# Last 64 score rows of two attention units at once, in quarters of the TensorE array

## The chip, the cores and the metric

The kernel runs on one core of a Trainium2 chip. The metric is the device time of one execution in microseconds. Three runs of the kernel before gave 938.68, 938.79 and 940.41 us; the median, 938.79 us, is the time that the change is compared with. All times here are microseconds unless ns is written.

## What is computed

Three stages follow one another. The first is attention with a memory, for B = 4 batches, H = 8 heads, S = 576 tokens and D = 64:

```python
scores = scale * np.matmul(q, k.transpose(0, 1, 3, 2))
scores = np.where(causal, -1000000000.0, scores)
a = np.exp(scores - scores.max(-1, keepdims=True))
a /= a.sum(-1, keepdims=True) + 1e-09
local = np.matmul(a, v)
q_p = np.where(q > 0, q, np.exp(q) - 1.0) + 1.0
mem_out = einsum(q_p, M_prev) / (einsum(q_p, z_prev)[..., None] + 1e-06)
g = 1.0 / (1.0 + np.exp(-beta))
x = g * mem_out + (1 - g) * local
```

The result is laid out as 2304 tokens x 512. Then `softplus(x @ w_in) @ w_out` with a hidden width of 2048, and then `((x @ w_a) * (x @ w_b)) @ w_out2` with a hidden width of 1536. All of it is fp32; the inputs of the attention and w_in are drawn with a spread 8 times larger than usual.

## The kernel before, in words

**A planner orders everything.** The program does not issue instructions as it is written. Each call (`PE.matmul`, `V.tensor_tensor`, `SP.dma_start`, ...) records a `Step` in a `Plan`. `Plan.weigh` (L157) gives each step a cost in a model of the chip, and `Plan.order` (L207) plays the steps through a list schedule: of what is ready, each engine takes the step with the largest `rank`, the longest modelled way to the end; PE takes its steps strictly in program order inside a stream. Stream 0 is the attention and has precedence over stream 1, the two dense stages. The result is one fixed order for each of PE (TensorE), DVE (VectorE), ACT (ScalarE), POOL (GpSimd) and SP (the queue that issues the DMAs). On the chip each engine keeps to this order and waits where a semaphore makes it wait; a step that is late holds up all that stands behind it on its engine. For DMAs of SP the planner has one limit, `LANES` (L33, L241): it issues the next one only when the sixth last one has landed in the model. DMAs on ACT's queue have no such limit.

**Attention** (`attention`, L657, and `Unit`, L454). A unit is one batch and two heads; there are 16, and the two heads hold the two halves of the 128 partitions. The loop runs over n = 0 to 17 and works on three units at once: `cur` = unit n, `prev` = unit n-1, `old` = unit n-2. In program order one turn of the loop is:

- `cur.score` (L504): q k^T of the first 512 rows, in tiles of 128 rows. q and k are each split into two fp32r parts (`qh`, `ql`, `kh`, `kl`), and three products are added up. The two heads use the upper and the lower half of the array at the same time (64*128). DVE then masks and takes the maximum (L514), ACT exponentiates and sums (L518).
- `prev.memory` (L547): phi(q) times M and z, in plain fp32, which is two instructions for one matmul.
- `nxt.prep_k` (L472): POOL and ACT split q and k of the next unit. SP loads unit n+2 (`loads_k`, L458) into one of two buffers each for `kr` and `qr`, and v.
- `old.use` and `old.finish` (L619, L635 to L652): probabilities times v, times the softmax scale that lies in `rb`, and the store to `xs`.
- `cur.score_tail` (L522): the last 64 rows. The two heads' q stand in one 128x128 block with zeros outside the diagonal (`qt[..., 512:640]`, L1171 to L1175), so that the whole array gives both heads: two chunks of 288 columns, three fp32r products each, six matmuls a unit (L531). Then one DVE pass (L532) and one ACT pass (L536).
- `cur.sums`, `cur.over` (L574, L579): POOL adds 1e-9 to the sums, DVE inverts them: `rs`, one column for each block of rows.
- `prev.send` (L558): PE turns `rs` (L562), DVE copies it (L563), SP stores it to DRAM (`rsd`, L565) and loads it back spread over 64 partitions for each head (`rb`, L568).
- `prev.turn` five times and `prev.turn_tail`: PE turns the probabilities (L589, L606, L607), ACT or DVE copies them out of PSUM (L595, L597, L609). The PSUM banks for this are the ring 4, 5, 2, 3.
- `prev.spread` (L627): the memory part is turned into the output's bank.

**The dense stages** read `xs` back, split it into fp32r parts (`right_parts`, L766) and multiply by a seven-product scheme (`Seven`, L807; L850 is its matmul). The weights come as raw 64-bit words: `decode` (L725) loads one matrix part of 1 MB with one DMA and unpacks it on DVE and ACT. `left_parts` (L755) does this for `w_in`; the first two are worked on POOL (`e` = G), their raw loads stand on ACT's DMA queue and wait for the second unit's q split (`begun`). All others load on SP.

Of the kernel before, what the change touches and what calls it, by code (L numbers as in the profile page):

```python
# [9 lines left out]
F32 = mybir.dt.float32  # L10
# [21 lines left out]
START, CONST, WORDS = 6272, 1280, 55680  # L32
SWITCH, LANES = 190, 6  # L33

# [18 lines left out]
class Plan:  # L53
# [153 lines left out]
    def order(self):  # L207
# [22 lines left out]
        while done < len(steps):  # L230
            nxt = float("inf")
            moved = False
            for e in engines:
# [4 lines left out]
                if free[e] > t:  # L238
                    nxt = min(nxt, free[e])
                    continue  # L240
                if e == "SP" and now[e] and len(landed) >= LANES and landed[-LANES] > t:  # L241
                    nxt = min(nxt, landed[-LANES])
                    continue
# [74 lines left out]
def tile_kernel(ctx: ExitStack, tc: tile.TileContext, qt, kt, vt, mz, be, w_in, w_out, w_a, w_b, w_2, out):  # L318
# [72 lines left out]
    early, late, spare = space(X1), space(X2), space(SUMS)  # L391
    for n, words in (("kr", S), ("qr", 640), ("qh", 640), ("ql", 640), ("kh", S), ("kl", S), ("ph", 640)):
        put(n, words, early(words), early(words), dtype=F32R if n[1] in "hl" and n != "ph" else F32)
    put("pos", 640, early(640))
    w3 = [early(512) for _ in range(3)]
    put("eTrue", 512, *w3, spare(512), *(late(512) for _ in range(4)))
    put("eFalse", 256, *(spare(256) for _ in range(4)), *(late(256) for _ in range(4)))
    put("eT", 640, spare(640), late(640))
    put("vr", 640, late(640), spare(640), spare(640))
# [32 lines left out]
    def gates():  # L432
        A.activation(out=gt, in_=bt, func=AF.Exp, scale=-1.0)
        G.tensor_scalar(out=gt, in0=gt, scalar1=1.0, scalar2=1.0, op0=ALU.mult, op1=ALU.add)
        V.reciprocal(out=gt, in_=gt)
        pairs = gt.rearrange("p (n j) -> p n j", j=2)
        for j, r in enumerate(both):
            rnd(G, gp[r], pairs[r, :, j])
        G.tensor_scalar(out=og, in0=gt, scalar1=-1.0, scalar2=1.0, op0=ALU.mult, op1=ALU.add)
# [13 lines left out]

    class Unit:  # L454
        def __init__(self, b, p):
            self.b, self.p = b, p

        def loads_k(self):  # L458
# [13 lines left out]
        def prep_k(self, first=False):  # L472
            kr, qr = self.kr, self.qr
            self.qh, self.ql, self.kh, self.kl = (take(n) for n in ("qh", "ql", "kh", "kl"))
            e = V if first else G
            for c, d in ((0, 256), (256, 640)) if first else ((0, 640),):
                k, q = slice(c, min(d, S)), slice(c, d)
                rnd(e, self.kh[:, k], kr[:, k])
                self.begun = {A.activation(out=self.qh[:, q], in_=qr[:, q], func=AF.Copy).n}
                sub(e, self.kl[:, k], kr[:, k], f(self.kh[:, k]))  # L480
                sub(e, self.ql[:, q], qr[:, q], f(self.qh[:, q]))
# [12 lines left out]
        def score(self, k, *rows):  # L494
# [4 lines left out]
            for i in rows:  # L499
                L = 128 * (i + 1)  # L500
                qc = slice(128 * i, 128 * i + 128)
                for t, (a, b) in enumerate(((qh, kh), (qh, kl), (ql, kh))):
                    for j, r in enumerate(both):
                        PE.matmul(  # L504
# [17 lines left out]
        def score_tail(self, k):  # L522
            qh, ql, kh, kl, sm, mn, Es = self.qh, self.ql, self.kh, self.kl, self.sm, self.mn, self.E
            s = bank[:, k : k + 2]
            terms = ((qh, kh), (qh, kl), (ql, kh))
            e640 = take("eT")
            e = e640[:, 0:S]
            for c in range(2):
                cs = slice(288 * c, 288 * c + 288)
                for t, (a, b) in enumerate(terms):  # L530
                    PE.matmul(out=s[:, c, :288], lhsT=a[:, 512:640], rhs=b[:, cs], start=t == 0, stop=t == 2)  # L531
            V.tensor_tensor_reduce(  # L532
# [3 lines left out]
            A.activation(out=e, in_=e, func=AF.Exp, scale=-1.0, bias=mn[:, 4:5], accum_out=sm[:, 4:5])  # L536
            Es["t"] = e640

        def memory(self, k):
# [5 lines left out]
            for c in range(5):  # L545
                for j, r in enumerate(both):
                    PE.matmul(  # L547
# [84 lines left out]
        def finish(self):  # L632
# [16 lines left out]
            while done < S:  # L649
# [3 lines left out]
                done += n  # L653

    order = [Unit(b, p) for b in range(B) for p in range(NP)]

    def attention():  # L657
# [16 lines left out]
        for n in range(nu + 2):  # L674
            cur, prev, old, nxt = (at(n - d) for d in (0, 1, 2, -1))
            if cur:
                cur.begin()
                cur.score(2, 2)
                cur.score(0, 0, 1)
                cur.score(4, 3)  # L680
# [17 lines left out]
            if cur:  # L698
                cur.score_tail(0)
                cur.sums()  # L700
                cur.over()
            if prev:
                rings["psT"][1] = 0
                if old:
                    prev.send(bank[0:10, 3, 0:128])
                prev.turn(A, [(0, 0)])
# [4 lines left out]
                prev.turn_tail()  # L711
                if not old:
                    prev.send(bank[0:10, 3, 0:128])
                prev.spread()

    attention()


# [5 lines left out]

    def decode(src, to, step=4, q=SP):  # L725

        raw = take("raw").bitcast(U32).rearrange("p (m c) -> p m c", c=2)
        q.dma_start(out=raw, in_=src).deps.update(order[1].begun if q is A else ())
        four = lambda t: t.rearrange("p (b n) -> p b n", b=4)
# [25 lines left out]
    def left_parts(src, at, e=V):  # L755

        w, d = (t.rearrange("p (n h m) -> p n h m", n=7, h=2) for t in twice("w", 3584, at))
        d = d[:, :, 1]
        decode(src, d[:, 0:4], 2, SP if e is V else A)
        left_sums(*(d[:, n] for n in range(7)), e)  # L760
# [447 lines left out]
```

## Time and profile before

| | us |
|---|---|
| median of three runs (lowest, highest) | 938.79 (938.68, 940.41) |
| the profiled execution, its own time | 940.39 |
| its span in the trace | 938.6 |
| PE busy in the span | 922.6 (98%) |
| DVE busy | 791.1 (84%) |
| ACT busy | 566.8 (60%) |
| POOL busy | 103.0 (11%) |

The profiled execution's span is read from the first to the last event on the core; 1.8 us lie outside it. "Busy" of PE is the time in which at least one matmul is in flight; matmuls overlap, so two that run at once count once. PEclk is the clock that TensorE was granted, as a share of 2.4 GHz. In the chain and wait views an arrow names what released an instruction. Queue names: SPq and ACTq are the sequencers of SP and ACT issuing DMAs.

### The profile page before, as it was taken

What the parts mean: (1) busy time and instruction counts of PE and PEld (TensorE: products, weight loads), DVE (VectorE), ACT (ScalarE), POOL (GpSimd) and SP (SyncE); (2) the same over time, 40 slices, a digit from 0 to 9 for tenths busy, and PEclk for the clock granted to TensorE, in tenths of its full rate; (3) what the DMA queues carried; (4) which work ended last, traced back from release to release, by engine and by line L of the source; (5) the groups of instructions that cost most, each with busy time, mean ns of one, the idle gap of its engine ahead of it and who ended that gap; (6) DMA issues with size and microseconds to landing.
All of it is one profiled execution on the core that took longest, in us unless ns stands there. A gap on an engine that the chain in (4) does not pass through costs nothing.

```text
span 938.6 us, 16918 instructions
## 1 busy us (share of the span) xinstructions
PE 922.6 (98%) x6204; PEld 890.1 (95%) x6204; DVE 791.1 (84%) x1503; ACT 566.8 (60%) x1124; POOL 103.0 (11%) x137
## 2 busy tenths in 40 slices
PE   7989999999999999999999999999999999999998
PEld 6878788899999999999999999999999999999998
DVE  7969989979998946998679999999997566998683
ACT  8968999757766756754446555544444334555452
POOL 6434588200000000000000000000000000000000
PEclk9999999999999999999999999999999999999999
DMA  6654564376988899482641444466654146672701
GB/s 185 193 162 131 169 186 130 99 232 215 312 292 293 267 329 370 172 299 73 202 135 34 134 157 159 159 226 208 224 188 144 43 160 192 245 234 74 225 32 50
DMA packets 81378, 172.10 MB, mean 183 GB/s; under 512 B 7936, under 2 KB 60560, under 8 KB 76048
## 3 DMA queue, kind: packets, MB, share of 16 engines
q1 hardware_dynamic: 80576, 168.61, 54.4%
q10 hardware_dynamic: 720, 2.43, 0.7%
q8 instruction: 48, 0.79, 0.3%
q14 instruction: 34, 0.28, 0.1%
HBM read 110.90 MB, written 60.10 MB: 182 GB/s over the span
## 4 chain that ended last, share of the span: by engine, by line
PE 86%; DVE 5%; ACT 3%; DMA 3%; issue 1%; POOL 1%; SPq 0%; DVEq 0%; POOLq 0%; ACTq 0%
PE bank L850 46%; PE bank L994 33%; DMA rb<-rsd 2%; PE bank L619 1%; PE bank L504 1%; PE bank L589 1%; PE bank L547 1%; DVE eTrue L514 1%; ACT eTrue L518 1%; PE bank L531 1%; ACT eFalse L518 1%; DMA kr<-kt 1%; PE bank L606 1%; PE bank L627 0%; ACT aT L595 0%
## 5 line engine op out<-in xcount | busy, mean ns | idle before, releaser
L340 DVE TENSOR_TENSOR s<-bank,s 128x384 f32<-128x384 f32 x216 | 117.2, 552 | 44.9 <-PE bank L850 38.9
L828 ACT ACTIVATE s<-bank 128x384 f32<-128x384 f32 x72 | 35.1, 487 | 73.2 <-PE bank L850 43.1
L337 DVE TENSOR_TENSOR t<-t,t 128x1536 f32<-128x1536 f32 (+1 forms) x48 | 74.5, 1552 | 0.4
L850 PE MATMUL bank<-x1h,w 128*128 128x384 f32 x240 | 71.0, 335 | 0.0
L850 PE MATMUL bank<-x6h,w 128*128 128x384 f32 x240 | 70.7, 335 | 0.3 <-ACT s L825 0.3
L850 PE MATMUL bank<-x5h,w 128*128 128x384 f32 x240 | 70.5, 334 | 0.0
L850 PE MATMUL bank<-x2h,w 128*128 128x384 f32 x240 | 70.5, 334 | 0.0
L850 PE MATMUL bank<-x3h,w 128*128 128x384 f32 x240 | 70.5, 334 | 0.0
L850 PE MATMUL bank<-x7h,w 128*128 128x384 f32 x240 | 70.5, 334 | 0.0
L850 PE MATMUL bank<-x4h,w 128*128 128x384 f32 x240 | 70.5, 334 | 0.0
L330 ACT ACTIVATE w<-wf 128x256 fp32r<-128x256 f32 (+1 forms) x100 | 50.0, 500 | 20.4 <-DVE w L337 16.4
L886 ACT ACTIVATE s<-s 128x384 f32<-128x384 f32 x72 | 37.2, 523 | 33.0 <-DVE s L340 32.9
L825 ACT ACTIVATE s<-bank 128x384 f32<-128x384 f32 x72 | 35.1, 487 | 35.8 <-PE bank L850 22.9
L330 ACT ACTIVATE gx2h<-t 128x768 fp32r<-128x768 f32 x37 | 31.4, 848 | 35.9 <-PE bank L994 32.7
L337 DVE TENSOR_TENSOR w<-wf,w 128x256 fp32r<-128x256 f32 (+1 forms) x90 | 47.2, 525 | 5.5 <-ACT w L330 4.9
L330 ACT ACTIVATE gx1h<-t 128x768 fp32r<-128x768 f32 x37 | 31.3, 846 | 33.4 <-PE bank L994 33.4
L734 ACT ACTIVATE raw<-raw 128x512 f32<-128x512 f32 (+1 forms) x54 | 42.6, 802 | 12.4 <-DVE raw L733 12.1
L330 ACT ACTIVATE gx0h<-t 128x768 fp32r<-128x768 f32 x37 | 31.3, 846 | 29.4 <-PE bank L994 28.5
L337 DVE TENSOR_TENSOR gx0l<-t,gx0h 128x768 fp32r<-128x768 f32 x37 | 35.3, 954 | 14.2 <-ACT gx0h L330 13.9
L518 ACT ACTIVATE eTrue<-eTrue,mn 128x384 f32<-128x384 f32 (+1 forms) x64 | 42.1, 660 | 8.2 <-DVE mn L514 8.0
L337 DVE TENSOR_TENSOR gx1l<-t,gx1h 128x768 fp32r<-128x768 f32 x37 | 35.3, 954 | 13.2 <-ACT gx1h L330 13.1
L831 ACT ACTIVATE s<-bank 128x384 f32<-128x384 f32 x72 | 35.1, 488 | 18.6 <-PE bank L850 14.6
(344 smaller groups left out, 3040.7 us busy)
## 6 DMA issues: line engine op xcount, KB each, us to landing
gs<-s SPq DMA_DIRECT2D x96, 192.0 KB
t<-gs SPq DMA_DIRECT2D x24, 768.0 KB
us<-s SPq DMA_DIRECT2D x72, 192.0 KB
t<-us SPq DMA_DIRECT2D x12, 768.0 KB
raw<-w_out SPq DMA_DIRECT2D x8, 1024.0 KB
raw<-w_in SPq DMA_DIRECT2D x6, 1024.0 KB
raw<-w_a SPq DMA_DIRECT2D x6, 1024.0 KB
raw<-w_b SPq DMA_DIRECT2D x6, 1024.0 KB
```

Source lines behind the costliest of these rows:

```text
L330: A.activation(out=o, in_=i, func=AF.Copy)
L337: eng.tensor_tensor(out=o, in0=a, in1=b, op=ALU.subtract)
L340: eng.tensor_tensor(out=o, in0=a, in1=b, op=ALU.add)
L504: PE.matmul(out=s[:, j, at : at + L], lhsT=a[r, qc], rhs=b[r, 0:L], start=t == 0, stop=t == 2, skip_group_check=True,)
L518: A.activation(out=e, in_=e, func=AF.Exp, scale=-1.0, bias=mn[:, n : n + 1], accum_out=sm[:, n : n + 1])
L734: A.activation(out=f(high), in_=f(high), func=AF.Identity, scale=REBIAS)
L825: A.activation(out=self.s1, in_=bank["b"], func=AF.Copy)
L828: A.activation(out=self.s5, in_=bank["c"], func=AF.Copy)
L831: A.activation(out=self.s2, in_=bank["b"], func=AF.Copy)
L850: PE.matmul(out=o, lhsT=w(n, a, k), rhs=x[n][c][:, k], start=start and k == t == 0, stop=k == 1 and t == 2, skip_group_check=True,)
L886: A.activation(out=s, in_=s if bank is None else bank, func=AF.Softplus)
L994: PE.matmul(out=o, lhsT=self.w[n][a][:, u, 128 * m : 128 * m + 128], rhs=x[c][:, j], start=start and u == t == 0, stop=u == self.nu - 1 an ...
```

## The change

It is one change in five parts.

1. `score_tail` no longer multiplies. A new function `tails` computes the last 64 rows of two units, n and n+1, at once, in every even turn of the loop. It uses `qr` and `kr` as loaded, in plain fp32, and gives each head of each unit a quarter of the array (64 rows x 64 columns). For an odd unit the heads change halves of q, k, memory and v input (`self.rows`), so that the four quarters are all different. The two units write to banks 0, 1 and 4, 5, the two heads of a unit to the two halves of the same bank.
2. In odd turns there is no tail. `qh` and `ql` shrink from 640 to 512 columns; `kr` and `qr` get a third buffer each, `eT` a third.
3. An odd unit's `send` stands at the end of its own turn of the loop. An even unit's stays where it is. The PSUM banks of the turning follow a ring of six that differs between even and odd turns, and the two `send`s use banks 0 and 5 in place of 3.
4. `decode` loads the raw weights in pieces: four of 256 KB for the first two `w_in` parts, which now stand on SP without the wait for `begun`; two of 512 KB for the other weights that are split in place; the weights that are spilled to DRAM are still loaded whole.
5. The planner gets a second limit for SP: when the most urgent DMA is a large one (over 300 ns of transfer in the model), it is held back while the modelled transfers already queued reach over 500 ns ahead.

```diff
-SWITCH, LANES = 190, 6
+SWITCH, LANES, AHEAD = 190, 6, 500
+TAIL = 4
+SEND, SENDC = 0, 5
+RINGS = [2, 3, 0, 1, 4, 5], [4, 5, 2, 3, 0, 1]
...
+                if e == "SP" and now[e] and steps[now[e][0][1]].size > 300 and lane[e] > t + AHEAD:
+                    nxt = min(nxt, lane[e] - AHEAD)
+                    continue
...
-    for n, words in (("kr", S), ("qr", 640), ("qh", 640), ("ql", 640), ("kh", S), ("kl", S), ("ph", 640)):
-        put(n, words, early(words), early(words), dtype=F32R if n[1] in "hl" and n != "ph" else F32)
+    more = space(WL + 7168)
+    for n, words in (("kr", S), ("qr", 640), ("qh", 512), ("ql", 512), ("kh", S), ("kl", S), ("ph", 640)):
+        at = [early(words), early(words)] + [more(words)] * (n in ("kr", "qr"))
+        put(n, words, *at, dtype=F32R if n[1] in "hl" and n != "ph" else F32)
...
-    put("eT", 640, spare(640), late(640))
+    put("eT", 640, spare(640), late(640), spare(640))
...
-        for j, r in enumerate(both):
-            rnd(G, gp[r], pairs[r, :, j])
+        for odd in range(2):
+            for j, r in enumerate(both):
+                rnd(G, gp[r, odd::2], pairs[r, odd::2, j ^ odd])
...
+            self.rows = [(h, both[h ^ (p & 1)]) for h in range(2)]
...
         def score_tail(self, k):
...
-            for c in range(2):
-                cs = slice(288 * c, 288 * c + 288)
-                for t, (a, b) in enumerate(terms):
-                    PE.matmul(out=s[:, c, :288], lhsT=a[:, 512:640], rhs=b[:, cs], start=t == 0, stop=t == 2)
...
+    def tails(at):
+        for c in range(2):
+            for u, k in at:
+                for j, r in u.rows:
+                    PE.matmul(
+                        out=bank[both[j], k + c, :288], lhsT=u.qr[r, 512 + 64 * j : 576 + 64 * j], rhs=u.kr[r, 288 * c : 288 * c + 288],
+                        start=True, stop=True, skip_group_check=True,
+                    )
+        for u, k in at:
+            u.score_tail(k)
...
             if cur:
-                cur.begin()
+                if n % 2 == 0:
+                    cur.begin()
...
             if cur:
-                cur.score_tail(0)
+                if n % 2 == 0:
+                    nxt.begin()
+                    tails(((cur, 0), (nxt, TAIL)))
                 cur.sums()
                 cur.over()
             if prev:
-                rings["psT"][1] = 0
-                if old:
-                    prev.send(bank[0:10, 3, 0:128])
+                rings["psT"] = [RINGS[n % 2], 0]
+                if n % 2:
+                    prev.send(bank[0:10, SEND, 0:128])
...
-                if not old:
-                    prev.send(bank[0:10, 3, 0:128])
                 prev.spread()
+                if cur and n % 2:
+                    cur.send(bank[0:10, SENDC, 0:128])
...
-    def decode(src, to, step=4, q=SP):
+    def decode(src, to, step=4, load=4):
         raw = take("raw").bitcast(U32).rearrange("p (m c) -> p m c", c=2)
-        q.dma_start(out=raw, in_=src).deps.update(order[1].begun if q is A else ())
+        for b in range(0, 1024, 256 * load):
+            m = slice(b, b + 256 * load)
+            SP.dma_start(out=raw[:, m], in_=src[:, m])
...
-        decode(src, d[:, 0:4], 2, SP if e is V else A)
+        decode(src, d[:, 0:4], 2, 2 if e is V else 1)
```

The host side changes to match: for odd units the heads' order is reversed in v, beta and the rows of w_in, and the last 64 rows of q change halves.

## Rows read from the trace of the kernel before

**Rows 1.** The page's first part: busy time, share of the span, instructions.

```profile
PE 922.6 (98%) x6204; PEld 890.1 (95%) x6204; DVE 791.1 (84%) x1503; ACT 566.8 (60%) x1124; POOL 103.0 (11%) x137
```

**Rows 2.** Stretches: busy time (instructions) of PE, PEld, DVE, ACT, POOL; clock; DMA share; GB/s.

```profile
80.00:90.00 10.00, 10.00 (x117) 8.44 (x116) 9.37 (x33) 7.94 (x24) 4.30 (x8) 1.00 0.46 150
...
150.00:160.00 10.00, 10.00 (x112) 8.21 (x112) 8.73 (x29) 10.00 (x29) 8.74 (x10) 1.00 0.54 167
200.00:300.00 100.00, 100.00 (x579) 100.00 (x578) 93.08 (x175) 69.32 (x140) 0.00 (x0) 1.00 0.84 277
```

**Rows 3.** Timeline of PE, the scale's turn (L562) of five loop turns: start, duration.

```profile
38.80 0.27 PE L562 MATMUL bank<-ident,rs 128*10 128x128 f32 x1
...
65.57 0.27 PE L562 MATMUL bank<-ident,rs 128*10 128x128 f32 x1
...
98.76 0.27 PE L562 MATMUL bank<-ident,rs 128*10 128x128 f32 x1
...
111.13 0.27 PE L562 MATMUL bank<-ident,rs 128*10 128x128 f32 x1
...
176.64 0.27 PE L562 MATMUL bank<-ident,rs 128*10 128x128 f32 x1
```

**Rows 4.** Timeline of PE, the last 64 rows of one unit.

```profile
27.12 0.40 PE L531 MATMUL bank<-kh,qh 128*128 128x288 f32 x1
27.36 0.29 PE L531 MATMUL bank<-kl,qh 128*128 128x288 f32 x1
...
28.02 0.27 PE L562 MATMUL bank<-ident,rs 128*10 128x128 f32 x1
```

**Rows 5.** Timeline of PE, other shares of the array.

```profile
24.12 2.37 PE L619 MATMUL bank<-aT,vr 128*64 128x512 f32 x16
26.32 0.64 PE L639 MATMUL bank<-aT,vr 128*64 128x64 f32 x16
...
33.18 0.39 PE L504 MATMUL bank<-kl,qh 64*128 64x512 f32 x2
33.41 0.40 PE L504 MATMUL bank<-kh,ql 64*128 64x512 f32 x2
```

**Rows 6.** Timelines of ACTq, SPq, DVE and PE around the first stall.

```profile
41.34 0.82 ACTq L728 DMA_DIRECT2D raw<-w_in  x2
...
42.92 1.25 SPq L568 DMA_DIRECT2D rb<-rsd  x2
...
52.78 0.69 DVE L635 TENSOR_TENSOR xx<-bank,rb 128x512 f32<-128x512 f32 x1 [1.47 <-DMA rb<-rsd]
...
54.76 0.33 PE L589 MATMUL bank<-ident,eFalse 128*128 128x128 f32 x1 [3.59 <-DVE rt L563]
```

**Rows 7.** Two stretches at the first stall, columns as in rows 2.

```profile
50.00:52.00 2.00, 1.17 (x11) 0.93 (x9) 0.22 (x1) 1.02 (x2) 0.00 (x0) 1.00 1.11 227
56.00:58.00 2.00, 2.00 (x11) 1.83 (x9) 1.05 (x3) 0.84 (x2) 1.79 (x3) 0.50 0.03 8
```

**Rows 8.** SP's own waits to 200 us; timelines of SPq and PE at the second stall.

```profile
SPq L463 <- POOL kl L337: 13.8, 7, 3.3
...
93.32 0.87 SPq L775 DMA_DIRECT2D raw<-xs  x1
94.28 1.09 SPq L568 DMA_DIRECT2D rb<-rsd  x2
...
103.25 0.33 PE L607 MATMUL bank<-ident,eT 128*128 128x128 f32 x1 [1.25 <-DVE xx L647]
```

**Rows 9.** Timelines of ACT, POOL and PE at the end of a loop turn.

```profile
37.95 0.19 ACT L518 ACTIVATION_READ_ACCUMULATOR eFalse<-eFalse,mn 128x1 f32 x1
...
41.20 1.55 POOL L337 TENSOR_TENSOR ql<-qr,qh 128x640 fp32r<-128x640 f32 x1
43.92 0.48 POOL L574 TENSOR_SCALAR ss<-sm 128x9 f32<-128x9 f32 x2 [1.18 <-DVE mn L514]
...
42.21 0.45 PE L504 MATMUL bank<-kh,qh 64*128 64x384 f32 x2
```

More of the change, by code (lines that the diff above doesn't have):

```diff
@@ L476, in prep_k @@
             for c, d in ((0, 256), (256, 640)) if first else ((0, 640),):
-                k, q = slice(c, min(d, S)), slice(c, d)
+                k, q = slice(c, min(d, S)), slice(c, min(d, 512))
                 rnd(e, self.kh[:, k], kr[:, k])
-                self.begun = {A.activation(out=self.qh[:, q], in_=qr[:, q], func=AF.Copy).n}
+                A.activation(out=self.qh[:, q], in_=qr[:, q], func=AF.Copy)
                 sub(e, self.kl[:, k], kr[:, k], f(self.kh[:, k]))
@@ L502, in score @@
                 for t, (a, b) in enumerate(((qh, kh), (qh, kl), (ql, kh))):
-                    for j, r in enumerate(both):
+                    for j, r in self.rows:
                         PE.matmul(
@@ L522, in score_tail @@
         def score_tail(self, k):
[L523 to L527, printed above, removed]
-            for c in range(2):
-                cs = slice(288 * c, 288 * c + 288)
-                for t, (a, b) in enumerate(terms):
-                    PE.matmul(out=s[:, c, :288], lhsT=a[:, 512:640], rhs=b[:, cs], start=t == 0, stop=t == 2)
+            s, e640 = bank[:, k : k + 2], take("eT")
+            e, mn, sm = e640[:, 0:S], self.mn, self.sm
             V.tensor_tensor_reduce(
@@ L536, in score_tail @@
             A.activation(out=e, in_=e, func=AF.Exp, scale=-1.0, bias=mn[:, 4:5], accum_out=sm[:, 4:5])
-            Es["t"] = e640
+            self.E["t"] = e640
         def memory(self, k):
@@ L545, in memory @@
             for c in range(5):
-                for j, r in enumerate(both):
+                for j, r in self.rows:
                     PE.matmul(
@@ L1173, with by_unit @@
     qt[..., 0:512] = turned[..., 0:512].reshape(B, NP, 128, 512)
-    for j in range(2):
-        qt[:, :, 64 * j : 64 * j + 64, 512 + 64 * j : 576 + 64 * j] = turned[:, :, j, :, 512:576]
+    for p in range(NP):
+        for j in range(2):
+            h = 64 * (j ^ (p & 1))
+            qt[:, p, 64 * j : 64 * j + 64, 512 + h : 576 + h] = turned[:, p, j, :, 512:576]
+    def by_unit(a, axis):
+        a = a.copy()
+        at = (slice(None),) * axis
+        a[at + (slice(1, None, 2),)] = a[at + (slice(1, None, 2), slice(None, None, -1))]
+        return a
     arrays = {
@@ L1178 @@
         "kt": arr(split(k).transpose(0, 1, 2, 4, 3).reshape(B, NP, 128, S)),
-        "vt": arr(split(v).transpose(0, 1, 3, 2, 4).reshape(B, NP, S, 128)),
+        "vt": arr(by_unit(split(v), 1).transpose(0, 1, 3, 2, 4).reshape(B, NP, S, 128)),
         "mz": arr(
@@ L1188 @@
         ),
-        "be": arr(inputs["beta"]),
-        "w_in": turn(pairs(kxm(inputs["moe_w_in"]))),
+        "be": arr(by_unit(inputs["beta"].reshape(NP, 2), 0).reshape(H)),
+        "w_in": turn(pairs(kxm(by_unit(inputs["moe_w_in"].reshape(NP, 2, D, DFF1), 0).reshape(DM, DFF1)))),
         "w_out": swap(pairs(inputs["moe_w_out"].reshape(-1, 128, DM))),
```

## The prediction

> **What bounds the kernel now.** I read the page first. TensorE is busy 98% of the span [rows 1], so a gain must either take work from PE or close one of its gaps. The stretches by ten and a hundred microseconds say where gaps are left: from 200 us on, in the dense stages, PE is busy 100.00 of 100 us [rows 2] (seven rows alike, to 900 us, the lowest 99.98). What the change does to loads there has no gap to close; it can only open one. All that can be won lies in the attention, before about 190 us.
>
> There the timeline of PE gives the pace. The scale's turn (L562) comes once in a loop turn. From 28.02 to 38.80 us one loop turn took 10.78 us [rows 4, 3] with PE never waiting; I take that as the price of a loop turn's work. From 38.80 to 176.64 us, 12 loop turns took 137.84 us [rows 3], 8.5 us more than 12 x 10.78 = 129.4. Two places hold most of it. Two loop turns from 38.80 to 65.57 took 26.77 us, 5.2 too many; one from 98.76 to 111.13 took 12.37, 1.6 too many [rows 3].
>
> The waits say what ended last there. At the first, ACT's queue issues two raw weight loads of 1 MB at 41.34 us, and 1.2 us later SP issues the two loads of `rb` for unit 2. DVE gets this scale at 52.78, nearly ten microseconds after issue, and the finish of the unit, which stands ahead of everything else on DVE, makes PE wait 3.59 us [rows 6]. In 50 to 52 us the DMA engines are full (share 1.11). After the gap TensorE's granted clock is 0.50 of 2.4 GHz, that is 1.2 GHz, in 56 to 58 us [rows 7], which is the rest of the 5.2 us. At the second place SP issues an `xs` load at 93.32, just ahead of `rb`, and PE waits 1.25 us at 103.25 for the DVE row that needs this `rb`. SP itself often comes late: seven times it stood at a `kr` load until POOL had split an older `kr`, 13.8 us in all and 3.3 at most, with everything behind it [rows 8].
>
> The other engines have little room: DVE is busy 9.37 of 10 us in a plain stretch, and ACT 10.00 from 140 to 170 us [rows 2] (three rows alike).
>
> **The change, part by part.**
>
> *The tail's work.* Before, one unit's six matmuls hold PE from 27.12 to 28.02, 0.90 us; the first takes 0.24, the other five 0.132 each, so 0.11 is the change of the array's division [rows 4]. An odd loop turn loses this but keeps a change of division (from column halves to the whole array): 0.79 saved. An even one gets 8 plain fp32 matmuls, 16 instructions of 288 columns, on quarters. No row shows quarters. The nearest is probabilities times v, also plain fp32, on column halves: 16 instructions with 5120 columns in all (512, 384, 256 and 128, each 4 times) from 24.12 to 26.32, 0.430 ns a column with two at a time [rows 5], so 0.86 ns alone. An instruction of 288 columns is then 0.248 us alone, 0.124 with two at a time, 0.062 with four. I take four, because each division that the trace has runs at its full count: column halves here, and row halves in the scores, where two matmuls of 512 columns start every 0.23 us [rows 5], 0.45 ns a column for the two. The tails are then 16 x 0.062 = 0.99, and I add 0.11 twice, for the division before and after: 1.21 in place of 0.90. A pair of units saves 0.79 - 0.31 = 0.48, eight pairs **3.8 us**. With the second change of division between nothing and twice 0.11, it is 2.9 to 4.7. Bounds of the whole term: 4.7 gained with four at a time, 20.0 lost with one at a time (16 x 0.248 + 0.22 = 4.19; 4.19 - 0.90 - 0.79 = 2.50 a pair).
>
> *The raw loads* move from ACT's queue to SP, eight issues for two, in pieces, with the planner's new limit ahead of them. A `rb` then has about one piece of 256 KB before it and not 2 MB. They have no input to wait for, so the planner can place them from the start; what is decoded from them is used in the dense stage only. SP pays about as much for an issue as ACT did (0.41 each [rows 6]), and its own waits [rows 8] cover six more. This removes the first stall: **5.2 us**, the gap with its slow clock; bounds 0 (the load of `rb` is late for another reason) and 5.2. Next in line there are DVE's passes, which cost a few tenths that I keep in the range.
>
> *The third `kr` and `qr`* take SP's waits for POOL [rows 8] away from ahead of `rb`. The `xs` load of 768 KB still stands there in one piece. I give **1.2** of the second stall's 1.6; bounds 0 and 1.6.
>
> *The odd unit's `send`* moves forward past a block of scores, with one transpose, one DVE copy and three DMAs; SP issues these ahead of the next unit's loads. Only odd units profit, and both stalls are of even units (2 and 6), whose `send` stays: nothing gained. What it could cost is a rival below.
>
> *Narrower `qh`, `ql`, more buffers and banks, more small steps at the gates*: 128 of 640 columns less on ACT and POOL (`ql` took 1.55 us [rows 9]), all beside PE's work: 0. The unit's DVE and ACT passes are as many as before, but come two in a row in even loop turns; bounded by one DVE pass that PE waits for (0.69 for one of 512 columns [rows 6]), 0.69 x 8 = 5.5 lost, against 0; I take 0, since the ring has six banks now.
>
> *What is not realized.* In the three stretches where ACT is full [rows 2], some three loop turns, PE's saving of 0.24 a turn is lost: 3 x 0.24 = **-0.7**. *Weights in two pieces and the new limit in the dense stages*: 0, under a full PE.
>
> **Sum.** The profiled execution took 940.39 us, span 938.6 and 1.8 around it. 3.8 + 5.2 + 1.2 - 0.7 = 9.5 gives 930.9. The median is 1.6 below this execution. If these 1.6 lie in its stalls, they are not won twice and the median run after is 930.9; if they lie elsewhere, 929.3. I say **930.0**.
>
> **Rivals.**
>
> *The stall is replaced* (S). DVE and ACT hold every loop turn near 10.8 us or a raw piece that DVE waits for comes late, so that the 5.2 come back as waits for DVE. For: DVE 9.37, ACT 10.00 [rows 2]. Against: turns without a PE wait exist in the same profile. 930.0 + 5.2 = 935.2.
>
> *Two at a time* (T). Both heads of a unit write to the same bank, from two row halves; before, two row halves always write to two banks (`s[:, j]`). If the two heads therefore take turns, the tails cost 16 x 0.124 + 0.22 = 2.20; a pair loses 2.20 - 0.90 - 0.79 = 0.51, eight pairs 4.1 in place of 3.8 gained: 930.0 + 7.9 = 937.9, no change to be measured.
>
> The Trainium skill, TensorEngine Tiling (Array Packing), section Restrictions and Gotchas, says just this: row tiles are to write to different PSUM banks and cannot use one bank at the same time. By that rule the result is T; no row of this trace has two row tiles in one bank, so the trace doesn't say.
>
> *The moved `send` waits* (W), the case on the other side. Place: the end of each odd loop turn, on PE, ahead of the next scores. It needs the last sum of that unit (ACT, done at 38.14 in the turn that ends at 42.21), two POOL steps (0.48) and DVE's inverse [rows 9]; about 0.7 us of work in 4.1, so it is hidden by 3.4 us. Price: if POOL's order puts the two sums behind the next unit's split, as before (`ql` ends at 42.75, sums from 43.92 [rows 9]), the scale is ready at about 43.5 at best, and PE stands 1.4 us in each of 8 odd turns: 11 us, 930.0 + 11.2 = 941.2, slower. It decides from 1.4 us a turn on. Against it: the planner sees the dependency, and ranks these two short steps above a split that is needed a turn later.
>
> *One at a time* (O): 930.0 + 23.8 = 953.8. Nothing in the trace speaks for it.
>
> **Chances.** Forecast 0.60, S 0.22, T 0.08, W 0.06, O 0.04. About 0.2% (1.9 us; the three runs span 1.7) can be told from no change, so faster means under 936.9 and slower over 940.7. Faster: the forecast and all but 0.03 of S, 0.79. Same: 0.03 of S and T, 0.11. Slower: W and O, 0.10. Range: below, all 8.5 us of excess gone, 4.7 from the tails and 0.3 for the four loop turns outside the twelve, 13.5 from 940.4 with the 1.6 off: 925.3, with a little for the first turns 924.5; above, S with its own spread, 937.0. T, W and O stay outside, 0.18.
>
> **What would show it.** In the profile after: 16 instructions of 64*64 and 288 columns in eight blocks, starting every 0.06 us (0.12 is T, 0.25 is O); no matmul of 128*128 with 288 columns; no PE gap of over 1 us between 40 and 110 us and the clock at 1.00 there; `rb` about 3 us after its issue; raw loads before 40 us on SPq; the twelve loop turns in some 128 us. The forecast is wrong if PE shows waits for DVE's `rs` or `rt` at the ends of odd turns (W), if loop turns stay at 10.8 with PE waiting for DVE (S), or if PE falls below 100 us in a hundred after 200 us, which I priced at nothing.

## The result, and the profile after

The kernel after the change took 931.14 us (median of four runs, 930.95 to 932.58), the kernel before 939.44 (four runs, 938.68 to 940.41). The ratio is 0.9914 with an interval of 0.9897 to 0.9932: 8.1 us faster, between 6.4 and 9.7. The forecast was 930.0. The total is close partly by luck: the loop won more than the sum said, and the start lost 5 us that the sum did not hold.

The page's first part, of after (it answers to [rows 1]):

```profile
PE 916.2 (99%) x6236; PEld 881.2 (95%) x6236; DVE 791.9 (85%) x1503; ACT 565.9 (61%) x1124; POOL 99.8 (11%) x140
```

Stretches of after, columns as in [rows 2]:

```profile
10.00:20.00 10.00, 6.00 (x56) 4.34 (x56) 7.54 (x29) 10.00 (x36) 7.68 (x15) 0.79 0.95 298
20.00:30.00 10.00, 10.00 (x91) 8.45 (x91) 8.66 (x30) 8.68 (x21) 4.65 (x6) 0.87 0.58 156
40.00:50.00 10.00, 10.00 (x117) 8.29 (x115) 9.90 (x33) 9.25 (x26) 3.43 (x5) 1.00 0.27 91
50.00:60.00 10.00, 10.00 (x129) 8.35 (x125) 9.85 (x31) 8.90 (x26) 4.53 (x9) 1.00 0.76 224
...
200.00:300.00 100.00, 100.00 (x579) 100.00 (x578) 94.23 (x182) 70.10 (x141) 0.00 (x0) 1.00 0.85 280
```

From 40 us on PE is full or nearly so (9.79 of 10 us at the least), also in 50 to 60 us, where before it stood 3.59 us [rows 6] and then had half the clock [rows 7]. The dense stages stay full (99.98 of 100 at the least). But from 10 to 20 us PE is busy 6.00 of 10 us, and the granted clock is 0.79 there and 0.87 in the next ten.

The timeline of PE, of after: start, duration, line, idle time ahead of it and what ended it.

```profile
17.95 2.40 PE L553 MATMUL bank<-mz,ph 64*128 64x65 f32 x20 [4.00 <-POOL ql L343]
...
24.90 0.44 PE L517 MATMUL bank<-kh,qh 64*128 64x384 f32 x2
...
31.18 1.20 PE L666 MATMUL bank<-kr,qr 64*64 64x288 f32 x16
32.31 0.44 PE L595 MATMUL bank<-ident,eFalse 128*128 128x128 f32 x2
...
35.75 0.44 PE L517 MATMUL bank<-kh,qh 64*128 64x384 f32 x2
...
45.59 0.72 PE L517 MATMUL bank<-kh,qh 64*128 64x384 f32 x2
...
161.30 0.44 PE L517 MATMUL bank<-kh,qh 64*128 64x384 f32 x2
```

Three of the same places in the timeline of PE, of before:

```profile
14.16 1.33 PE L547 MATMUL bank<-mz,ph 64*128 64x65 f32 x20 [0.58 <-POOL mz L447]
...
19.88 0.77 PE L504 MATMUL bank<-kh,qh 64*128 64x384 f32 x2
...
169.07 0.45 PE L504 MATMUL bank<-kh,qh 64*128 64x384 f32 x2
```

The 64x384 matmul of `kh` and `qh` is the first of a unit's scores, so its starts mark the loop turns. 19.88 and 24.90 belong to unit 2, 35.75 to unit 3, 45.59 to unit 4, 169.07 and 161.30 to unit 15. They cut the span in three:

| stretch | before | after | difference |
|---|---|---|---|
| to unit 2's first scores | 19.88 | 24.90 | +5.02 |
| unit 2 to unit 15 (13 turns) | 149.19 | 136.40 | -12.79 |
| the rest of the span | 769.53 | 768.00 | -1.53 |

So the steady loop won more than the 9.5 us of the sum, and the start lost 5.0, which no term of the sum held. An even turn now takes 10.85 (24.90 to 35.75), an odd one 9.84 (35.75 to 45.59).

Lines of after, the tails (count, minimum, median and maximum duration in ns, first and last start):

```profile
L666 PE MATMUL bank<-kr,qr x128: 402/403/453, 9.1 to 157.4; 64*64 64x288 f32 x128
```

Sixteen of these hold PE from 31.18 to 32.31, 1.13 us, 0.071 each; the forecast had 1.21. At the 0.248 for one alone they would take 3.97, so some 3.5 run at a time with the division's change counted in. Rivals T (2.20) and O (4.19) have fallen.

DMA issues of after: count, KB each, median us from issue to landing.

```profile
rb<-rsd SPq DMA_DIRECT2D x32, 144.0 KB, 3.1
```

SP's waits of after to 200 us: in all, times, longest.

```profile
SPq L477 <- POOL ql L343: 0.9, 2, 0.5
```

The timeline of SPq, of after:

```profile
13.80 2.33 SPq L751 DMA_DIRECT2D raw<-w_in  x5
...
25.84 0.56 SPq L751 DMA_DIRECT2D raw<-w_in  x1
```

`rb` lands 3.1 us after its issue, SP stands 0.9 us behind POOL's splits in place of 13.8 [rows 8], and the eight raw pieces lie between 13.8 and 26.4 us. S has fallen with the even turn's 10.85 and the odd one's 9.84; W too: the odd unit's `send` opens no gap of PE (no PE gap over 0.21 us from 18 to 180 us).

Why the start is late: the timelines of DVE and POOL, of after.

```profile
10.52 0.69 POOL L340 TENSOR_SCALAR kh<-kr 128x576 fp32r<-128x576 f32 x1
11.30 1.44 POOL L343 TENSOR_TENSOR kl<-kr,kh 128x576 fp32r<-128x576 f32 x1
...
15.90 1.27 POOL L343 TENSOR_TENSOR ql<-qr,qh 128x512 fp32r<-128x512 f32 x1
...
16.24 1.61 DVE L502 SCALAR_TENSOR_TENSOR ph<-ph,pos 128x640 f32<-128x640 f32 x1
```

The memory product of unit 0 (L553) needs `ph`. DVE ends it at 17.85, PE starts at 17.95. The profile puts the wait down to POOL's `ql`, but that was done at 17.17 already. In the timeline of DVE, of before, the same step runs early:

```profile
6.36 0.82 DVE L489 SCALAR_TENSOR_TENSOR ph<-ph,pos 128x640 f32<-128x640 f32 x1 [0.41 <-ACT pos L486]
```

PE's wait is 3.4 us longer than before (4.00 and 0.58). Most of the rest of the 5.0 is the clock: it stands at 0.50 (1.2 GHz) from 17.95 to 22.3 us, and the same twenty memory instructions take 2.40 there, 1.33 before at 1.00 (2.4 GHz).

### The profile page after: what moved, and what is told of

The parts are those of the page before. It is cut to its first block, busy times and chain, and to the rows that moved or that the text cites. A ratio compares the mean times of both kernels' runs of the same rounds, so it can differ in the third digit from the quotient of the medians.

```text
span 929.3 us, 17003 instructions
## 1 busy us (share of the span) xinstructions
PE 916.2 (99%) x6236; PEld 881.2 (95%) x6236; DVE 791.9 (85%) x1503; ACT 565.9 (61%) x1124; POOL 99.8 (11%) x140
## 4 chain that ended last, share of the span: by engine, by line
PE 95%; DVE 3%; issue 1%; ACT 1%; DMA 1%; POOL 0%; ACTq 0%; DVEq 0%; POOLq 0%
PE bank L873 47%; PE bank L1017 33%; PE bank L625 3%; PE bank L595 3%; PE bank L517 3%; PE bank L553 2%; PE bank L645 1%; PE bank L666 1%; PE bank L612 1%; PE bank L633 1%; DMA bt<-be 1%; DVE aT L603 0%; DVE ph L502 0%; DVE eTrue L527 0%; ACT eTrue L531 0%
## 5 line engine op out<-in xcount | busy, mean ns | idle before, releaser
L343 DVE TENSOR_TENSOR gx2l<-t,gx2h 128x768 fp32r<-128x768 f32 x37 | 35.3, 954 | 11.6 <-ACT gx2h L336 11.3
```

The lines of the kernel that those rows point to most:

```text
L343: eng.tensor_tensor(out=o, in0=a, in1=b, op=ALU.subtract)
```

## The experiments

Twelve kernels. In the expectations S, T, W and O are the rivals above. P says that phi of unit 0 is late because ACT's `exp` of the gate waits for its small load ahead of phi's two ACT passes; Q, that the planner gives the SBUF port, which its model shares out between DVE and POOL, to POOL's early splits; V, that the planner is blind to what ACT's DMA queue does to SP's transfers, for it counts each queue in a lane of its own (`lane[e]`). The columns "unit 2" (its first scores) and "2 to 15" are of the profiled execution, whose own time stands beside them; the ratio is worked out from all executions of both kernels and can differ a little from that of the two medians.

| kernel | median | ratio to before, same chip | profiled | unit 2 | 2 to 15 |
|---|---|---|---|---|---|
| before | 939.44 | | 940.39 | 19.88 | 149.19 |
| after | 931.14 | 0.9914 [0.9897, 0.9932] | 931.10 | 24.90 | 136.40 |
| e1 gate behind phi | 932.18 | 0.9916 [0.9903, 0.9929] | 932.99 | 26.51 | 136.58 |
| e2 split behind phi | 930.27 | 0.9899 [0.9886, 0.9912] | 930.66 | 23.60 | 137.43 |
| e3 old loads | 931.34 | 0.9905 [0.9890, 0.9919] | 931.37 | 25.23 | 136.27 |
| e4 new loads only | 935.31 | 0.9953 [0.9939, 0.9966] | 938.16 | 20.84 | 146.28 |
| e5 two buffers | 931.54 | 0.9899 [0.9885, 0.9914] | 931.21 | 23.77 | 138.08 |
| e6 send late | 936.58 | 0.9958 [0.9941, 0.9974] | 935.07 | 24.68 | 140.12 |
| e8 tails only | 935.63 | 0.9944 [0.9931, 0.9957] | 936.39 | 25.32 | 141.10 |
| e10 phi first | 929.50 | 0.9884 [0.9869, 0.9900] | 928.74 | 21.52 | 137.58 |
| e11 burst on SP | 931.72 | 0.9898 [0.9883, 0.9912] | 931.98 | 25.73 | 136.39 |
| e12 burst on ACT | 941.41 | 1.0003 [0.9988, 1.0017] | 938.19 | 24.71 | 143.79 |
| e13 whole on SP | 938.56 | 0.9978 [0.9967, 0.9988] | 939.04 | 20.82 | 147.12 |
| e14 send late, bank 7 | 936.60 | 0.9960 [0.9947, 0.9973] | 937.36 | 26.97 | 139.31 |

### The start: e1, e2 and e10

**e1**, after with the gate's `exp` held back behind unit 0's first ACT pass of phi:

```diff
-        A.activation(out=gt, in_=bt, func=AF.Exp, scale=-1.0)
+        A.activation(out=gt, in_=bt, func=AF.Exp, scale=-1.0).deps.add(order[0].relu)
```

> The changed kernel, with one dependency more: the exponential of the gate (ACT) waits until phi's two passes of unit 0 are through. Theory P (the first memory matmul starts 4 us late because ACT takes the gate's exponential first and stands for the load of beta, so that phi comes too late for DVE's place for it): ACT doesn't stand at about 5 us, phi of unit 0 is on DVE before 8 us, PE's gap of 4.0 us at 14 to 18 us falls under 1.5 us and the granted clock is 1.00 from 20 us on; time 926 to 928 us against 931.1. Theory Q (the third buffer of kr lets POOL split unit 2 at once and keeps DVE from phi): the gap stays within 1 us of 4.0 and the time within 1 us of 931.1.

Timelines of DVE and PE, of e1:

```profile
16.83 1.61 DVE L502 SCALAR_TENSOR_TENSOR ph<-ph,pos 128x640 f32<-128x640 f32 x1
...
18.54 2.40 PE L553 MATMUL bank<-mz,ph 64*128 64x65 f32 x20 [4.09 <-POOL ql L343]
```

ACT had both its passes done by 6.43, and DVE still took its step at 16.83. P falls: it is not the input that is late, it is the step's place in DVE's order.

**e2**, after with POOL's split of unit 2 held back behind phi of unit 0:

```diff
+                if self is order[2]:
+                    plan.steps[-1].deps.add(order[0].phi)
...
```

> The changed kernel, with one dependency more: POOL's split of unit 2 waits for phi of unit 0. Theory P (ACT's order and the load of beta): phi of unit 0 comes at most 2 us sooner, since ACT still stands for beta; the gap of 4.0 us stays over 2 us, time 929 to 931. Theory Q (POOL's early split of unit 2): phi moves to about 9 us, the gap goes under 1.5 us, time 926 to 928.

Timelines of DVE and PE, of e2:

```profile
13.34 0.78 DVE L504 SCALAR_TENSOR_TENSOR ph<-ph,pos 128x640 f32<-128x640 f32 x1
...
16.24 1.33 PE L555 MATMUL bank<-mz,ph 64*128 64x65 f32 x20 [1.90 <-POOL mz L456]
```

Phi came 2.9 us sooner and the gap halved; the memory product now waited for POOL's `mz`. Unit 2 began 1.30 sooner than in after. The clock fell here too, to 0.50 from 18.5 to 21 us. Q holds in direction, but one split is not all of it.

**e10**, after with unit 1's split on POOL behind phi of unit 0, unit 2's behind the first gated memory `mz`, and unit 0's phi recorded ahead of unit 1's split:

```diff
+                if self is order[1]:
+                    plan.steps[-1].deps.add(order[0].phi)
+                if self is order[2]:
+                    plan.steps[-1].deps.add(plan.last["mz"])
...
+        order[0].prep_v()
+        order[0].prep_v2()
         order[1].prep_k()
-        order[0].prep_v()
...
```

> The changed kernel with two dependencies for POOL: unit 1's split waits for phi of unit 0, and unit 2's split for the first gated memory. Theory (POOL holds the port that it shares with DVE from 7 to 13 us in the planner's order, so DVE's place for phi of unit 0 comes only at 16 us; this made the 4.0 us gap and the slow clock behind it): phi of unit 0 is on DVE before 9 us, the first memory matmul starts before 15.5 us in place of 17.95, the granted clock is 1.00 from 20 us on, the third unit's scores start at 20 to 21.5 us in place of 24.90; 926 to 929 us. Rival (what the start wins is given back, since other engines set the loop turns): scores start earlier, but the time stays within 1 us of 931.1.

Timelines of DVE and PE, of e10:

```profile
7.32 0.82 DVE L508 SCALAR_TENSOR_TENSOR ph<-ph,pos 128x640 f32<-128x640 f32 x1
...
15.35 1.33 PE L559 MATMUL bank<-mz,ph 64*128 64x65 f32 x20 [0.98 <-POOL mz L456]
...
21.52 0.45 PE L523 MATMUL bank<-kh,qh 64*128 64x384 f32 x2
```

The gap of 4.00 became 0.98, the clock stayed at 1.00, unit 2 began 3.38 sooner than in after, and 2.2 of that were left at unit 15 (159.10 against 161.30). The ratio, 0.9884, is the lowest of all, 11 us under the kernel before. Under the kernel after it is 1.6 us by the medians and 2.8 by the ratios, whose intervals overlap, so that the gain of the whole run over after is likely and not certain. By e2 and e10 together, POOL's splits, placed first, kept phi back. That the planner placed them so because of the port is read from its code; e10 also changed the order in which the steps are recorded, and no run separates the two.

### The raw loads: e4, e3, e13, e11 and e12

**e4**, before with the loads in pieces on SP and the planner's new limit, nothing else:

```diff
+                if e == "SP" and now[e] and steps[now[e][0][1]].size > 300 and lane[e] > t + AHEAD:
+                    nxt = min(nxt, lane[e] - AHEAD)
+                    continue
...
-        q.dma_start(out=raw, in_=src).deps.update(order[1].begun if q is A else ())
+        for b in range(0, 1024, 256 * load):
+            m = slice(b, b + 256 * load)
+            SP.dma_start(out=raw[:, m], in_=src[:, m])
```

> The kernel before with only the loads changed: raw loads in pieces on SP and the planner's second limit; tails, buffers and send as before. Forecast's step: the stall at 50 to 58 us goes, 5.2 us less: 934 to 935 us; the second stall (1.6 us near 100 us) may stay. Rival (the loads alone don't cure it, since SP still stands at kr): the stall stays over 2 us, 938 to 940 us.

Timeline of PE, of e4, its gaps over 0.25 between 38 and 110 us:

```profile
41.76 0.33 PE L592 MATMUL bank<-ident,eFalse 128*128 128x128 f32 x1 [0.49 <-DVE rt L566]
...
98.94 0.33 PE L592 MATMUL bank<-ident,eFalse 128*128 128x128 f32 x1 [1.94 <-DVE rt L566]
```

The 3.59 at 54.76 [rows 6] is gone. 0.0047 of 939.93 is 4.4 us won, though the start lost 0.96: 5.4 for the loop. (This profiled execution is the slowest of its six, 2.9 above the median. It has 1.94 at the place of the second stall and another 1.09 at 121.63; whether the other five have these waits, no trace shows.)

**e3**, after with the old loads (whole, on ACT's queue, behind `begun`, no limit):

```diff
-SWITCH, LANES, AHEAD = 190, 6, 500
+SWITCH, LANES, AHEAD = 190, 6, 1e9
...
-            SP.dma_start(out=raw[:, m], in_=src[:, m])
+        q.dma_start(out=raw, in_=src).deps.update(order[1].begun if q is A else ())
```

> The changed kernel with the raw loads as before: whole, the first two on ACT's queue behind the second unit's split, and without the planner's second limit; tails, buffers and send stay changed. Forecast's step (the two loads of 1 MB ahead of rb made the stall of 5.2 us): a PE gap of over 2 us with DVE waiting for rb comes back between 30 and 70 us, time 934 to 937 us. Rival (the third buffer or the earlier send of odd units cured it, or the shorter loop turns moved it): no gap over 1 us after 20 us, time within 1 us of 931.1.

Timeline of ACTq, of e3:

```profile
31.20 0.33 ACTq L749 DMA_DIRECT2D raw<-w_in  x1
...
40.74 0.34 ACTq L749 DMA_DIRECT2D raw<-w_in  x1
```

No loss: in the changed order the two loads are issued 9.5 us apart, where before they went together [rows 6], and no gap follows. Its time is that of after (931.34 and 931.14). So in the changed order the new loads are worth nothing that can be measured, and whole loads on ACT's queue do not by themselves make a stall. What a pair just ahead of `rb` does there is left to e11 and e12.

**e13**, before with the first two loads whole on SP, without limit:

```diff
-        q.dma_start(out=raw, in_=src).deps.update(order[1].begun if q is A else ())
+        SP.dma_start(out=raw, in_=src)
```

> The kernel before with one edit: the first two raw loads on SP without the wait for the second unit's split, still whole, and without the second limit. Theory V: the queue is what matters; the loads go out before 20 us in the planner's sight, the stall at 50 to 58 us is gone as with the pieces, 934 to 936 us. Rival (pieces and limit did it): rb stands behind a load of 1 MB somewhere before 60 us, a PE gap of 2 us or more, 938 to 941 us.

Timelines of SPq, DVE and PE, of e13:

```profile
9.77 0.43 SPq L728 DMA_DIRECT2D raw<-w_in  x1
12.09 0.44 SPq L728 DMA_DIRECT2D raw<-w_in  x1
...
31.75 1.50 DVE L733 SCALAR_TENSOR_TENSOR raw<-raw 128x512 uint32<-128x512 uint32 x1
33.17 0.21 DVE L647 TENSOR_TENSOR xx<-bank,rb 64x64 f32<-64x64 f32 x1
...
34.27 0.33 PE L607 MATMUL bank<-ident,eT 128*128 128x128 f32 x1 [3.17 <-DVE xx L647]
```

The stall at 54 us is gone, another of 3.17 stands at 34 us, and half of e4's gain is lost. Each landed 7.6 us after its issue, so by 20 us; what comes early with them is their unpacking on DVE (L733), which stands ahead of the finish (`xx`) that PE waits for and makes up 1.50 of the 3.17. The new stall is one of the order, not of the transfers. Out of ACT's queue alone is not enough; in this kernel V does not explain the gain by itself.

**e11** puts both whole loads on SP at once, in the changed kernel without its second limit, just ahead of `rb`; **e12** the same on ACT's queue (the first line is e11's, the second e12's):

```diff
+        SP.dma_start(out=raw, in_=src).deps.update(order[2].early if q is A else ())
...
+        q.dma_start(out=raw, in_=src).deps.update(order[2].early if q is A else ())
```

> The changed kernel with the first two raw loads whole and issued together between the store and the loads of unit 2's scale, as they fell in the kernel before (there by chance of the order, here by a dependency); no second limit. The run with the old loads had them 9.5 us apart and had no stall, so it did not put the forecast's step to the test. Forecast's step (2 MB right ahead of rb make the stall): rb lands 8 to 11 us after issue, a PE gap of 2 us or more near 50 us with DVE waiting for rb, the granted clock under 1.00 behind it, 934 to 937 us. Rival (the shorter loop turns and the other buffers leave the scale enough time): rb lands as late, but no PE gap over 1 us, 930 to 932 us.

> As the burst run (whole raw loads behind unit 2's first turned probabilities, no second limit), but on ACT's queue, whose transfers the planner counts in a lane of their own. In the burst run rb came about 9 us after issue and PE lost only 1.0 us: the planner knew that SP's lane was full and had put DVE's passes over rb behind other work. Theory V (the stall of before comes from what the planner can't see, not from the 2 MB as such): the planner now puts those passes early, DVE stands for rb 2 us or more, PE has a gap of 2 us or more before 62 us, 933 to 936 us. Rival (the loop turns of the changed kernel leave the scale enough time anyway): no gap over 1.2 us, 930 to 932 us.

Timelines of SPq, DVE and PE, of e11:

```profile
45.50 0.83 SPq L751 DMA_DIRECT2D raw<-w_in  x2
...
47.48 1.11 SPq L574 DMA_DIRECT2D rb<-rsd  x2
...
56.57 0.68 DVE L643 TENSOR_TENSOR xx<-bank,rb 128x512 f32<-128x512 f32 x1
...
57.67 0.33 PE L615 MATMUL bank<-ident,eT 128*128 128x128 f32 x1 [0.99 <-DVE xx L655]
```

Timelines of ACTq, SPq, DVE and PE, of e12:

```profile
44.58 0.33 ACTq L751 DMA_DIRECT2D raw<-w_in  x1
...
49.69 1.46 SPq L574 DMA_DIRECT2D rb<-rsd  x2
...
54.25 0.69 DVE L643 TENSOR_TENSOR xx<-bank,rb 128x512 f32<-128x512 f32 x1 [1.82 <-DMA rb<-rsd]
...
55.67 0.33 PE L595 MATMUL bank<-ident,eFalse 128*128 128x128 f32 x1 [1.79 <-DVE mn L538]
...
115.57 2.40 PE L553 MATMUL bank<-mz,ph 64*128 64x65 f32 x20 [3.14 <-DVE ph L502]
```

With the pair on SP the planner knew of it and put the finish later, at 56.57, where DVE waited for nothing that the trace shows; PE lost 0.99 and the time stayed at 931.72, so e11 came out as its rival, against the forecast's step. With the pair on ACT's queue it put the finish as if `rb` came in time, DVE stood 1.82 for it and PE 1.79. This is the stall of before made again at half its size, and V explains the wait for `rb`. It is not the whole loss of e12: 6.3 us of its profile are one turn at 110 us (17.08 for 10.79), where phi is placed late once more, an accident of the new order. By the ratios 9.9 us lie between e11 and e12; their profiled executions, of which e12's is 3.2 under its median, hold 6.2 of them.

### The third buffer and the tails: e5 and e8

**e5**, after with two buffers for `kr` and `qr`; **e8**, before's loads, two buffers and the old place of the `send`, with the tails of after. In these two kernels the next loads overwrite `kr` and `qr` ahead of the tails, so that the last 64 rows in even turns are worked from a later unit's q and k, and the tails wait for that unit's load; the work is the same in kind and amount.

```diff
-        at = [early(words), early(words)] + [more(words)] * (n in ("kr", "qr"))
+        at = [early(words), early(words)]
```

> The changed kernel with two buffers for kr and qr, as before. Theory (POOL takes the port that it shares with DVE because unit 2 is loaded early, so phi of unit 0 comes late): POOL can't split unit 2 at 10 us, phi of unit 0 is done before 14 us, and the gap of 4.0 us at 14 to 18 us is under 2 us; the forecast's 1.2 us for SP's waits at kr would be lost: 928 to 930 us. Rival (the third buffer does no harm at the start and helps later): gap still 4 us and waits of SP at kr back, 932 to 934 us.

> The changed kernel with only the tails in quarters (and the rings of banks and the bookkeeping that they need): raw loads whole, the first two on ACT's queue, no second limit, two buffers for kr and qr, and every send where it was. The forecast's term for the tails: 3.8 us less than before if both stalls stay, 936 us; by the loop turns measured in the changed kernel (10.85 and 9.84 in place of 10.78 each) nearer 0.4 a turn, 6 us, 934 us. If 930 to 932, loads, buffers and send together are worth nothing beside the tails.

e5 has no PE gap over 0.3 us from 46 to 159 us, and SP's waits at `kr` for POOL's splits have not come back. Its time is that of after. So the third buffer is there for the data of the tails, and the second stall [rows 8] goes without it.

e8 won 5.3 us though its start lost 5.44. Timelines of DVE and PE, of e8:

```profile
11.73 0.77 DVE L502 SCALAR_TENSOR_TENSOR ph<-ph,pos 128x640 f32<-128x640 f32 x1
...
11.60 1.31 PE L666 MATMUL bank<-kr,qr 64*64 64x288 f32 x16 [1.80 <-DMA kr<-kt]
```

That start is late in another way than the start of after. Phi runs at 11.73 (11.79 in e5), and the memory product behind it waits for nothing. The 1.80 (2.21 in e5) is a wait for unit 2's `kr`, issued at 6.94 into unit 0's buffer: it belongs to the two buffers, since unit 1's `kr` had landed by 6.34, when POOL began to split it. So with two buffers phi is not late; but what the tails alone cost at the start can't be read from e5 and e8. The loads and the `send` do not make phi late: PE still waits 3.98 there in e3 and 3.75 in e6, and e4 starts at 20.84.

e8 shows one thing more. It has the old loads, two buffers and the late `send`, and neither stall of before: from 30 to 160 us no PE wait is over 0.62. Its pair of raw loads goes out at 12.68 and 13.05, far ahead of unit 2's `rb`. The new order of the tails is enough to remove both.

### The place of the odd `send`: e6 and e14

**e6**, after with all `send`s at the place they had before, in banks 0 and 3; **e14** with bank 7 in place of 3:

```diff
-                if n % 2:
-                    prev.send(bank[0:10, SEND, 0:128])
+                if old:
+                    prev.send(bank[0:10, SEND if n % 2 else 3, 0:128])
...
-                if cur and n % 2:
-                    cur.send(bank[0:10, SENDC, 0:128])
```

> The changed kernel with the odd units' send back at the place of before, in the next loop turn. Forecast's step: the earlier send is worth nothing, 930 to 932 us, no new wait for rb over 0.5 us. Rival (with odd turns of under 10 us an odd unit's rb would come too late without it): DVE waits for rb in even loop turns, 933 us or more.

> The run with the odd units' send at its old place, with one difference: the turned scale of an odd unit goes to bank 7, which is free then, and not to bank 3, which the second turning needs. Theory (the 5 us that the late send cost are PE's waits of 0.4 to 0.7 us for DVE to empty bank 3, once in each even loop turn, and no rb came late): these waits go, even loop turns return to under 11.2 us, 930 to 932.5 us. Rival (the place itself costs, through DVE's copy and the order behind it): even loop turns stay at 11.4 us or more, 934 us or more.

Timelines of PE and DVE, of e6, at the end of an even turn:

```profile
97.19 0.28 PE L568 MATMUL bank<-ident,rs 128*10 128x128 f32 x1
...
97.29 0.76 DVE L538 CUSTOM_DVE_ANT_0 eT<-bank,mask 128x576 f32<-128x576 f32 x1 [0.66 <-PE bank L666]
...
97.97 0.27 DVE L569 COPY rt<-bank 9x128 f32<-9x128 f32 x1
...
98.30 0.44 PE L595 MATMUL bank<-ident,eFalse 128*128 128x128 f32 x2 [0.40 <-DVE rt L569]
```

The two tail passes of DVE come just when the `send` needs its copy `rt`; the copy waits behind one of them (0.76), and PE waits 0.40 to 0.74 for the bank, in seven even turns and once more at the end (0.67). Even turns took 11.4 to 12.0 in place of 10.8 to 11.4; the 13 turns together 3.7 more than in after. By the ratios the late place costs 0.0044 (e6) and 0.0046 (e14), 4.1 and 4.3 us, each uncertain by some 2. In e14 these bank waits are gone, but the 13 turns still took 2.9 more than in after, 1.17 of them one PE wait for the finish's `xx` at 35.51. So the bank is the smaller part (0.8 of 3.7) and the place itself the larger; by which waits it costs the rest, these runs don't settle.

## Why the prediction was right in sum and wrong in some of its steps

**The sum: close, in part by luck.** At the prediction's 10.78 us a turn, the 13 turns from unit 2 to unit 15 would take 140.1. Before took 149.2, of which 9.1 are excess; after took 136.4, which is 3.7 under the undisturbed loop. So all 9.1 of the excess went, where the sum took 6.4 (5.2 and 1.2), and the turns' work gave 3.7, where it had 3.8 less 0.7 for all sixteen. The rest of the span gave 1.5, and the start took back 5.0. That is 9.3 between the two profiled executions for the 9.5 of the sum.

**The tails' work, 3.8 us: right in size.** Sixteen quarters took 1.13 where the step said 1.21, and the 3.7 of the count by turns goes with it (with the rings and the narrower splits in it; the undisturbed turn is uncertain by some 0.1, which is 1.3 in the 13). In this trace two row halves wrote to one bank at a rate of 3.5 of four quarters.

By the Trainium skill, TensorEngine Tiling (Array Packing), section Restrictions and Gotchas, row tiles cannot use one PSUM bank at the same time; this trace doesn't agree, its 1.13 us for sixteen being half of the 2.20 that turns would take. The two heads also write to different partitions of the bank; whether the rule holds without that, no run here shows.

**The raw loads, 5.2 us: right for the kernel before, not needed in the changed one.** In the kernel before, the new loads alone won 5.4 in the loop (e4). The mechanism (2 MB ahead of `rb`) was right: e12 makes the stall again, and e11 shows that it is smaller when the planner sees the pair. But the tails' new order has no such stall with the old loads either (e3, e8). The step priced the stall as one of the loads; it was one of the loads in that order, so this term and the tails do not add up. That whole loads on SP would only move the stall (e13) it didn't say.

**The third `kr` and `qr`, 1.2 us: wrong in its cause.** The second stall did go, but it goes with two buffers as well (e5), and with the tails alone (e8); with the loads alone 1.94 stands at its place (e4). SP's waits for POOL were beside the path. What in the tails' order removed it was not isolated.

**The odd `send`, "nothing gained": the first failed step.** It was costed by the two stalls alone, both of even units. But the tails of two units put two DVE passes at the very place where an odd unit's `send` used to be copied, in an even turn. Moving it out is worth 4.1 to 4.3 us (e6, e14). This does not come on top of the sum: with the late `send` the 13 turns take 140.1, as long as 13 undisturbed turns of before, so the tails' 3.8 hold only because it moved. The step looked at the kernel before for who waits behind a `send`; it should have looked at what else the change sets beside it.

**"More small steps at the gates" at 0 and no term for the start: the second failed step.** 5.0 us were lost there. POOL's splits for the units 1 and 2 came ahead, and the planner, which in its code never lets DVE and POOL hold the SBUF port together, kept phi of unit 0 until 16.24. e10 got 3.4 of it back at unit 2. The late phi is not made by the loads (e3, e4) or the `send` (e6), and it is absent with two buffers (e5, e8): the third buffer, priced as a gain, goes with the loss. How much the tails add is open. The phrase "all beside PE's work" was true of the steady loop and was carried over to a start that has nothing beside it.

**The rest.** Two DVE passes in a row cost PE nothing in the steady loop, as taken, once the odd `send` was out of their way. The -0.7 for stretches in which ACT is full has its like in the even turns of units 12 and 14, 11.21 and 11.44 in place of 10.8, but what ended them was not isolated. The dense stages lost nothing. Of the signs named, the loop turns (12 in 125.6, from 35.75 to 161.30, for some 128), `rb`'s 3.1 us, the early raw loads, and the clock of 1.00 from 40 us came as written; that PE might lose at the start was not among them.

## What to carry to other kernels

Cut the span at the same step in both traces before the totals are compared: 8 us that fit the forecast were 13 won and 5 lost, and e10 got 3.4 of the 5 back at unit 2. Two parts that each remove the same stall don't add up: e4 and e8 both removed the first one, so each part is worth what the others leave for it. A move of one step is to be costed against the order that the rest of the change makes, not against the old one; and a term that is hidden in the steady loop is to be priced once more for the start, where little covers it. An order fixed ahead of time is only as good as its model of what lies outside its engine: a load on another queue, or a port given to steps that nobody needs yet, shows up as a wait far from its cause.

## What was unexpected of the hardware

- One DVE step (phi, 128x640, both inputs in SBUF) took 1.61 us in after and in e1, where POOL ran a two-input step for its first 0.93 us, and 0.77 to 0.82 in before, e2 and e5, where POOL ran nothing at that time. It lost nearly the whole overlap (some 0.8 of 0.93). In e10 phi came first (0.82), and POOL's step of 8 columns that began during it took 0.49 in place of 0.20. In e13 the unpacking (L733), beside POOL's `kl`, took 1.50 in place of 0.69. The Trainium skill, SBUF — State Buffer, section Who interferes with whom, says that the shared port pair is an exclusive lock; these rows agree.
- The fall of the clock after a stall cost about as much as a small stall: twenty instructions took 2.40 us after the 4.00 gap, at a clock of 0.50, and 1.33 after gaps of 0.58, 0.98 and 1.90, at 1.00. The fall can come later: in e2 the clock was still 1.00 behind the 1.90 gap and stood at 0.50 from 18.5 to 21 us. With gaps of under 1.0 us from 12 us on, e10 kept 1.00 throughout.
